# Second block of an attention and expert kernel: the six weight steps of a visit, each one step later

## The chip, the cores and the metric

The kernel runs on one core of a Trainium2 chip. The metric is the device time of one execution in microseconds (us). Before the change the median of three runs is 888.69 us (887.83 to 889.95).

## What is computed

A linear attention with random features is followed by a mixture of four experts. Batch 4, 8 heads, 576 positions, head size 64, 128 features. For queries and keys, `phi(x) = exp(h - max h)` with `h = x omega^T - |x|^2/2`; then `kv = phi(k)^T v`, `z = sum phi(k)`, and the attention output is `phi(q) kv / (phi(q) z + 1e-6)`. The 2304 rows of 512 columns that result are the input `x` of the experts: with `p` the normalised `domain_probs`,

```
out = sum over e of p[:, e] * (max(x @ w1[e], 0) @ w2[e])      w1: 4 x 512 x 1024, w2: 4 x 1024 x 512, fp32
```

## The kernel before

Every operand of a large product is split into a high and a low part (`hi` a rounded copy made by ScalarE, `lo` the rest, made by GpSimd or VectorE), and a product is three matmuls: high by high, high by low, low by high.

The experts' work is cut into visits: a block of rows times one half of one expert's hidden columns (8 halves). The first block of rows is done plainly (visits 0 to 10). The second block has 768 rows and the third 1024; both use a scheme of seven products in place of eight on 2 by 2 blocks, in `fast(v)`. Visits 11 to 18 are those of the second block, 19 to 26 ("deep") those of the third.

One visit of the second block runs in this order on TensorE (lines 1095 to 1170): products `p1(0) p2(0) p5(0) p6(0) p1(1) p2(1) p7(0) p5(1) p3(0) p4(0) p6(1)`, then `begun(0)`, `p7(1)`, `begun(1)`, `p3(1)`, `p4(1)`, `begun(2)`, and then six output tiles. A product is six matmuls of 384 columns (line 934), for chunk 0 or 1 of the hidden columns. An output tile is twelve matmuls of 512 columns (lines 753 to 755); `begun(t)` does the first six of tiles 0 to 2 early. Each product lands in a PSUM bank (eight banks, one pool for everything). `keep` (L940, ScalarE) copies `p1` out of a bank before `p6` is accumulated into that same bank; `both` (L946 on VectorE adds, L955 on ScalarE takes the positive part, L959 on VectorE the low part) makes the hidden operands. `gather` (L782, VectorE; L780, ScalarE, the first time) adds a finished tile to the output rows.

Beside this, three things are threaded in by hand; every engine works strictly in the order in which the code emits:

- `sides(v + 1)`, a generator with six steps (`ready`), which makes the next visit's operands of `w1` out of the two raw tiles `w1r`. `direct(0)` and `direct(1)` split three blocks of a raw tile as they are (`w1ah` by ScalarE L564, `w1al` by GpSimd L567); `add(0)`, `add(1)` make four combinations in place (four VectorE additions, L684 to L687); `summed(0)`, `summed(1)` split those (`w1sh` by ScalarE, `w1sl` by GpSimd) and then issue, on the queue of SP, one load of a raw `w1` tile for the visit after (L549). They run in the order `direct(0) direct(1) add(0) summed(0) add(1) summed(1)`. Each of the four operand tags has two buffers, one for each raw tile: `direct(0)` of the next visit writes where the operands of this visit lie.
- `keep_sides(v)` (L670), emitted after `p3(0)`: eight transfers that write this visit's operands from those same buffers to DRAM (`kept`), where the third block fetches them.
- `next(ticks)`: pieces of the attention of the last batch, some 1.2 a step, emitted at each `yield 1`, that is after `begun(2)` and after each output tile: projections, maxima (L282, L287), biases (L292, L293), exponentials (L299, L306), GpSimd squares (L251), reciprocals, loads.

Before the change the first step of `ready` runs between `p6(1)` and `begun(0)`, and the other five after output tiles 0 to 4; the call after tile 5 finds nothing left. In visit 18 (the last before the third block) the call ahead of `begun(0)` is not made.

Of the kernel before, what the change touches and what calls it, by code (L numbers as in the profile page):

```python
# [14 lines left out]
def attention_moe(ctx, tc, kT, qT, kd, qd, kn, qn, vn, omT, probs, w1, w2, out):  # L15
# [514 lines left out]
    DEEP = range(N0 + NV, len(visits))  # L530
# [361 lines left out]
    def fast(v):  # L892
# [6 lines left out]
        ready = sides(v + 1) if v + 1 < len(visits) else iter(())  # L899
# [78 lines left out]
        def p6(g):  # L978
            product(g, 6, "u", start=False)
            keep(g, "u", "u2")  # L980
# [19 lines left out]
        def begun(t):  # L1000
            g2[t] = bank("g2")
            outputs(v, hs, g2[t], t, range(2))
# [142 lines left out]
        if v + 1 == DEEP[0]:  # L1145
            start_sides2(v + 1)
        p6(1)
        if v + 1 != DEEP[0]:
            next(ready, None)
        begun(0)  # L1150
        p7(1)
        begun(1)
# [226 lines left out]
    def emit():  # L1379
        pairs, g1 = begin()  # L1380
        later = [Halves(b, hp) for b in range(1, B) for hp in range(NP)]
        windows = {
            0: (first_rest(pairs, opening(later[0], both=True)), 15 / 11),
            3: (joint_ticks(later[:-NP]), 76 / 45.4),
            N0: (chain(opening(later[-NP]), later_ticks(later[-NP:])), 54 / (NV * (BIG[1][1] // P + 1) * 0.8)),
        }
        ticks, n, done, per = iter(()), 0, 0.0, 0
        for v in range(len(visits)):
            if v in windows:
                for _ in ticks:  # L1390
                    pass
                ticks, per = windows[v]
                n, done = 0, 0.0
            for share in first_visit(g1) if v == 0 else fast(v) if v >= N0 else plain(v):
                done += share
                while n < done * per:
                    next(ticks, None)
                    n += 1
        store(0)
# [61 lines left out]
```

## Time and profile before

| | us |
|---|---|
| median of three runs | 888.69 |
| lowest, highest | 887.83, 889.95 |
| the profiled execution | 889.82 |
| its span, first to last instruction | 888.0 |
| granted TensorE clock | 1.000 |

The profile is of one execution. PE is TensorE's matmuls, DVE VectorE, ACT ScalarE, POOL GpSimd, SP the queue that issues most transfers (its instructions have names such as SPq). Times in the rows are from the start of the span; "L940" is a line of the kernel. A bracket at the end of a timeline row gives the idle time of the engine ahead of the row and what ended it.

### The profile page before, as it was taken

The numbers are of one execution on the slowest core, as the hardware profiler recorded it, in microseconds if no ns is written. First come the engines' busy times: TensorE is split into PE (matmuls) and PEld (weight loads), VectorE is DVE, ScalarE is ACT, GpSimd is POOL, SyncE is SP. The second block draws the span as 40 slices with busy tenths as digits, with TensorE's granted clock in tenths as the row PEclk, the third lists the DMA queues.
The fourth block names the chain that finished last, engine by engine and source line by source line (L and its number), as shares of the span: only waits on it lengthen the run. The fifth ranks groups of instructions, "written<-read, shape, count | busy, mean of one in ns | idle before, by whom it ended". The sixth has DMA issues, their size and how long they took to land.

```text
span 888.0 us, 14766 instructions
## 1 busy us (share of the span) xinstructions
PE 878.8 (99%) x5484; PEld 789.4 (89%) x5484; DVE 590.9 (67%) x1025; ACT 470.2 (53%) x1039; POOL 563.7 (63%) x494
## 2 busy tenths in 40 slices
PE   9999999999999989999999999999999999999998
PEld 9988888989888888989888899899989898998988
DVE  5765566666677556576766756975858476675847
ACT  6554677776774555555554554544443434444442
POOL 6656465555644454443545346779898887979874
PEclk9999999999999999999999999999999999999999
DMA  7675345444521847536375354644152442415132
GB/s 183 164 223 158 110 161 176 128 137 139 183 72 48 297 123 262 198 131 236 88 262 169 116 213 160 235 152 154 60 178 75 149 155 86 155 60 179 46 121 95
DMA packets 64296, 134.01 MB, mean 151 GB/s; under 512 B 10368, under 2 KB 20800, under 8 KB 64224
## 3 DMA queue, kind: packets, MB, share of 16 engines
q1 hardware_dynamic: 54256, 102.95, 35.3%
q0 software_dynamic: 9360, 29.82, 10.4%
q8 instruction: 43, 0.70, 0.3%
q10 hardware_dynamic: 608, 0.30, 0.1%
q14 instruction: 29, 0.24, 0.1%
HBM read 98.96 MB, written 34.08 MB: 150 GB/s over the span
## 4 chain that ended last, share of the span: by engine, by line
PE 92%; DVE 3%; DMA 2%; issue 1%; POOL 1%; ACT 1%; SPq 0%; POOLq 0%; ACTq 0%
PE g L934 28%; PE g L1009 18%; PE g L753 8%; PE g L755 7%; PE g L754 7%; PE g L738 3%; PE g L739 3%; PE g L740 3%; PE kv L317 2%; PE q_ps L266 1%; PE k_ps L266 1%; PE qt_ps L328 1%; PE k_ps L147 1%; DMA kept<-w1ah 1%; PE q_ps L147 1%
## 5 line engine op out<-in xcount | busy, mean ns | idle before, releaser
L782 DVE SCALAR_TENSOR_TENSOR acc<-g,pr,acc 128x256 f32<-128x256 f32 (+1 forms) x278 | 139.2, 540 | 37.0 <-PE g L755 27.5
L567 POOL TENSOR_TENSOR w2l<-w2r,w2h 128x512 fp32r<-128x512 f32 x61 | 79.3, 1305 | 80.4 <-ACT w2h L564 68.2
L567 POOL TENSOR_TENSOR w1sl<-w1r,w1sh 128x512 fp32r<-128x512 f32 (+1 forms) x43 | 75.1, 1747 | 64.3 <-ACT w1sh L564 53.4
L753 PE MATMUL g<-w2h,hh 128*128 128x512 f32 x280 | 112.0, 400 | 1.8 <-DVE sum L946 1.6
L755 PE MATMUL g<-w2h,hl 128*128 128x512 f32 x280 | 109.7, 392 | 0.0
L754 PE MATMUL g<-w2l,hh 128*128 128x512 f32 x280 | 109.5, 391 | 0.0
L959 DVE SCALAR_TENSOR_TENSOR hl<-sum,hh 128x384 fp32r<-128x384 f32 (+1 forms) x64 | 48.3, 757 | 81.5 <-ACT hh L955 71.7
L946 DVE TENSOR_TENSOR sum<-g,sum 128x384 f32<-128x384 f32 (+1 forms) x96 | 59.3, 619 | 61.2 <-PE g L934 52.8
L934 PE MATMUL g<-xbh,w1sh 128*128 128x384 f32 (+1 forms) x256 | 93.1, 364 | 2.4 <-ACT sum L940 2.4
L934 PE MATMUL g<-xbl,w1sh 128*128 128x384 f32 (+1 forms) x256 | 92.9, 363 | 0.0
L934 PE MATMUL g<-xbh,w1sl 128*128 128x384 f32 (+1 forms) x256 | 92.6, 362 | 0.0
L940 ACT ACTIVATE sum<-g 128x384 f32<-128x384 f32 (+1 forms) x96 | 52.1, 543 | 69.2 <-PE g L934 68.3
L567 POOL TENSOR_TENSOR w1al<-w1r,w1ah 128x512 fp32r<-128x512 f32 (+1 forms) x45 | 51.4, 1157 | 52.2 <-ACT w1ah L564 35.4
L934 PE MATMUL g<-xbh,w1ah 128*128 128x384 f32 (+1 forms) x192 | 70.0, 365 | 0.0
L934 PE MATMUL g<-xbl,w1ah 128*128 128x384 f32 (+1 forms) x192 | 69.6, 362 | 0.0
L934 PE MATMUL g<-xbh,w1al 128*128 128x384 f32 (+1 forms) x192 | 69.5, 362 | 0.0
L753 PEld LDWEIGHTS g<-w2h,hh 128*128 128x128 f32 x280 | 52.6, 188 | 12.7 <-DVE sum L946 2.2
L755 PEld LDWEIGHTS g<-w2h,hl 128*128 128x128 f32 x280 | 52.5, 188 | 11.8 <-DVE hl L992 0.4
L754 PEld LDWEIGHTS g<-w2l,hh 128*128 128x128 f32 x280 | 52.6, 188 | 9.0
L955 ACT ACTIVATE hh<-sum 128x384 fp32r<-128x384 f32 (+1 forms) x64 | 35.0, 548 | 43.9 <-DVE sum L946 43.5
L934 PEld LDWEIGHTS g<-xbh,w1sh 128*128 128x128 f32 x256 | 48.1, 188 | 8.4 <-ACT sum L940 2.7
L934 PEld LDWEIGHTS g<-xbl,w1sh 128*128 128x128 f32 x256 | 48.1, 188 | 5.1
(214 smaller groups left out, 2475.3 us busy)
## 6 DMA issues: line engine op xcount, KB each, us to landing
w1r<-in_w SPq DMA_DIRECT2D x54, 512.0 KB, 3.6
w2r<-in_w SPq DMA_DIRECT2D x76, 256.0 KB, 2.9
kept<-w1sh SPq DMA_DIRECT2D x16, 512.0 KB, 5.0
kept<-w1sl SPq DMA_DIRECT2D x16, 512.0 KB, 5.5
w1sh<-kept POOLq DMA_DIRECT2D x16, 512.0 KB, 4.7
w1sl<-kept POOLq DMA_DIRECT2D x16, 512.0 KB, 5.6
kept<-w1ah SPq DMA_DIRECT2D x16, 384.0 KB, 5.1
kept<-w1al SPq DMA_DIRECT2D x16, 384.0 KB, 5.0
```

Source lines behind the costliest of these rows:

```text
L567: lo.tensor_tensor(c, t, f32(a), ALU.subtract)
L738: nc.tensor.matmul(ps[:, :n], a[:, w], hi, start=(hp == 0), stop=False)
L753: nc.tensor.matmul(ps, ha[:, ts_], wa, start=(c == 0), stop=False)
L754: nc.tensor.matmul(ps, ha[:, ts_], wc, start=False, stop=False)
L755: nc.tensor.matmul(ps, hc[:, ts_], wa, start=False, stop=(c == FH - 1))
L782: nc.vector.scalar_tensor_tensor(to, ps, sc, to, ALU.mult, ALU.add)
L934: nc.tensor.matmul(ps, a[:, w], x[:, k], start=(start and k + at == 0), stop=(k == 1 and at == 2), skip_group_check=not start)
L940: nc.scalar.activation(t, P_[g][where], AF.Copy)
L946: nc.vector.tensor_tensor(t, P_[g][where], t, ALU.add)
L955: nc.scalar.activation(ha, t, AF.Relu)
L959: nc.vector.scalar_tensor_tensor(x, y, 0.0, f32(z), ALU.max, ALU.subtract)
L1009: nc.tensor.matmul(to, x, w, start=(start and f + k == 0), stop=(f + k == 3), skip_group_check=not start)
```

## The change

In visits 11 to 17 the call between `p6(1)` and `begun(0)` is taken out. As a step is still taken after every output tile, the same six steps now run after tiles 0 to 5: each comes one place later, with all that it issues (two ScalarE copies and two GpSimd subtractions for each `direct`, four VectorE additions for each `add`, one ScalarE copy, one GpSimd subtraction and one SP load for each `summed`). Visit 18 is as it was. TensorE's own order doesn't change.

```
         p6(1)
-        if v + 1 != DEEP[0]:
-            next(ready, None)
         begun(0)
         p7(1)
         begun(1)
```

## Rows read from the trace of the kernel before

**Rows 1.** Windows, three lines: visit 12, visit 16, the sum over visits 11 to 18
```profile
317.20:357.32 40.12, 37.75 (x217) 33.85 (x215) 22.99 (x42) 22.25 (x54) 18.15 (x13) 1.00 0.56 191
...
468.80:506.85 38.05, 36.45 (x205) 32.23 (x204) 24.82 (x44) 19.03 (x46) 15.47 (x12) 1.00 0.45 152
...
sum 286.35, PE 282.19 PEld 252.47 DVE 188.28 ACT 153.18 POOL 138.18; mean PE 35.27 PEld 31.56 DVE 23.53 ACT 19.15 POOL 17.27
```

**Rows 2.** Timeline of TensorE, visit 16 (start us, duration us, engine, line)
```profile
486.38 0.34 PE L934 MATMUL g<-xbh,w1al 128*128 128x384 f32 x1
488.32 0.50 PE L753 MATMUL g<-w2h,hh 128*128 128x512 f32 x1 [1.60 <-DVE sum L946]
488.66 0.40 PE L754 MATMUL g<-w2l,hh 128*128 128x512 f32 x1
```

**Rows 3.** Chain of work ahead of that matmul (start us, us, what)
```profile
479.82 5.14 DMA kept<-w1ah
...
486.45 1.34 DVE hl L959
487.79 0.48 DVE sum L946
```

**Rows 4.** Timeline of ScalarE, visit 16
```profile
485.07 0.94 ACT L564 ACTIVATE w1ah<-w1r 128x512 fp32r<-128x512 f32 x2 [3.68 <-DMA kept<-w1ah]
```

**Rows 5.** Timeline of VectorE, visit 16
```profile
483.27 0.56 DVE L946 TENSOR_TENSOR sum<-g,sum 128x384 f32<-128x384 f32 x1 [2.34 <-PE g L934]
```

**Rows 6.** Groups by form, visits 11 to 17 (xcount | busy us, mean ns | idle, releasers)
```profile
L564 ACT ACTIVATE w1ah<-w1r 128x512 fp32r<-128x512 f32 x14 | 8.9, 634 | 18.4 <-DMA kept<-w1ah 18.4
...
L564 ACT ACTIVATE w1sh<-w1r 128x1024 fp32r<-128x1024 f32 x14 | 14.8, 1060 | 19.4 <-issue 13.0 <-DVE w1r L687 6.4
...
L567 POOL TENSOR_TENSOR w1sl<-w1r,w1sh 128x1024 fp32r<-128x1024 f32 x14 | 34.2, 2442 | 37.5 <-ACT w1sh L564 27.6 <-issue 5.3 <-PE qt_ps L328 4.6
...
L687 DVE TENSOR_TENSOR w1r<-w1r 128x256 f32<-128x256 f32 x14 | 6.0, 425 | 0.5
...
L782 DVE SCALAR_TENSOR_TENSOR acc<-g,pr,acc 128x512 f32<-128x512 f32 x36 | 26.4, 739 | 12.1 <-PE g L755 11.9
...
L940 ACT ACTIVATE sum<-g 128x384 f32<-128x384 f32 x42 | 20.6, 491 | 14.3 <-PE g L934 13.6
```

**Rows 7.** Timeline of TensorE, visit 15
```profile
448.42 0.34 PE L934 MATMUL g<-xbh,w1al 128*128 128x384 f32 x1
448.75 0.50 PE L753 MATMUL g<-w2h,hh 128*128 128x512 f32 x1
```

**Rows 8.** Timeline of TensorE, visit 11
```profile
304.03 0.39 PE L754 MATMUL g<-w2l,hh 128*128 128x512 f32 x1
304.42 0.50 PE L755 MATMUL g<-w2h,hl 128*128 128x512 f32 x1
```

**Rows 9.** Timeline of TensorE, start of visit 12
```profile
322.89 0.45 PE L934 MATMUL g<-xbh,w1sh 128*128 128x384 f32 x1 [2.37 <-ACT sum L940]
```

**Rows 10.** Timeline of VectorE ahead of it, visit 11
```profile
316.59 2.32 DVE L293 SCALAR_TENSOR_TENSOR nbk<-sqk,mxk 128x9 f32<-128x9 f32 x1
```

**Rows 11.** Timelines, end of visit 17 and start of visit 18: POOL, DVE, PE
```profile
536.42 2.68 POOL L567 TENSOR_TENSOR w1sl<-w1r,w1sh 128x1024 fp32r<-128x1024 f32 x1 [2.88 <-ACT w1sh L564]
...
536.88 2.50 DVE L685 TENSOR_TENSOR w1r<-w1r 128x256 f32<-128x256 f32 x1
...
536.82 0.39 PE L753 MATMUL g<-w2h,hh 128*128 128x512 f32 x1
...
539.54 0.33 PE L934 MATMUL g<-xbh,w1ah 128*128 128x384 f32 x1
...
542.69 0.33 PE L934 MATMUL g<-xbh,w1sh 128*128 128x384 f32 x1
...
546.85 0.33 PE L934 MATMUL g<-xbh,w1sh 128*128 128x384 f32 x1
```

**Rows 12.** Chain of work over the whole span, the same transfer in visit 13
```profile
368.22 3.51 DMA kept<-w1ah
```

More of the change, by code (lines that the diff above doesn't have):

```diff
@@ L1147, in fast @@
         p6(1)
-        if v + 1 != DEEP[0]:
-            next(ready, None)
         begun(0)
```

## The prediction

> **What bounds the kernel now.** TensorE does. I read the windows by visit first: over visits 11 to 18 TensorE is busy 282.19 of 286.35 us, so 4.16 us of idle time is all that anything in these visits can win, and it lies in few places: visit 12 has 2.37 us of it and visit 16 has 1.60 [rows 1]. The rest is smaller than the profile counts as idle and must be read from starts: an unhindered product matmul follows the last after 0.175 us (18 of them between the start of visit 18 and its `p6(0)`, 542.69 - 539.54 [rows 11]), a tile matmul after 0.227 us (twelve between 536.82 and 539.54 [rows 11]).
>
> Then the stall of visit 16. The first matmul of `begun(2)` comes at 488.32, 1.94 us after the one ahead of it, released by VectorE's L946 [rows 2]. The chain behind it runs back over L959 to a transfer, `kept<-w1ah`, which is this visit's operand on its way to DRAM and took 5.14 us [rows 3]. Between the two is ScalarE: it stood 3.68 us with the two copies of `direct(0)` at its head, because they overwrite the buffer that this transfer reads [rows 4]. All ScalarE work behind them had to wait, first the positive part of `p7(1)`, whose sum VectorE had finished at 483.83 [rows 5]. VectorE, also in order, then did `p7(1)`'s low part (L959, 1.34 us from 486.45) ahead of `p3(1)`'s sum, and that sum frees the bank that `begun(2)` wants [rows 3]. In all ScalarE lost 18.4 us in nine such waits [rows 6]; most cost TensorE nothing, but visit 15 shows a start 0.33 us after the last and visit 11 one of 0.39 at the matmul that needs the last low part [rows 7, 8].
>
> The other stall, 2.37 us at `p6(0)` of visit 12, is of another kind: `keep` (L940) is late on ScalarE [rows 9], because the attention's exponentials stand ahead of it, which waited for a bias (L293) that took 2.32 us [rows 10].
>
> **The change, part by part.** It removes no instruction; six steps in each of visits 11 to 17 come one place later.
>
> *`direct(0)`, from before `begun(0)` to after tile 0.* The two copies leave the head of ScalarE at the critical place. By then `begun(0)` to `begun(2)`, three products and half a tile have passed: 18 product matmuls (3.15 us) and 24 tile matmuls (5.4 us), 8.6 us, more than the 5.14 us of the slowest transfer shown. So the wait is gone, not moved. In visit 16 `p7(1)`'s positive part could start at 483.83 instead of about 486.0 (485.07 + 0.94 [rows 4]), `p3(1)`'s sum follows its product, and `begun(2)` follows after 0.175. Gain: 488.32 - 486.38 - 0.175 = 1.77 us, and the slow first matmul behind the stall (488.66 - 488.32 = 0.34 against 0.227), 0.11 us [rows 2]. Visit 15: 0.33 - 0.175 = 0.16 us [rows 7]. Visit 11: 0.39 - 0.227 = 0.16 us [rows 8]. Together 2.20 us. On GpSimd the two `w1al` subtractions go along; they no longer run beside L959.
>
> *`direct(1)`, after tile 1, and `add(0)`, `summed(0)` after tiles 2 and 3.* I cost these at nothing. Cover: the next visit needs `w1ah` of chunk 1 only at `p1(1)`, more than four tiles of 2.72 us later. `summed(0)` (1.06 on ScalarE, then 2.44 on GpSimd [rows 6]) starts two tiles before the visit ends and is wanted at `p5(0)`, 12 matmuls into the next one: 5.4 + 2.1 = 7.5 us for 3.5 us of work. Without that cover each microsecond late would be one of TensorE's.
>
> *`add(1)` after tile 4, `summed(1)` after tile 5.* This is the tight one, and what is late next. `add(1)` follows tile 4's gather on VectorE: tile 4 ends 2.72 us before the visit does, the gather takes 0.74, the four additions 4 x 0.46 = 1.84 (0.425 and a gap of 0.5 / 14) [rows 6], so they end 0.1 us before the next visit starts. `summed(1)`'s copy (1.06) now stands on ScalarE straight ahead of the next visit's `keep` (0.49), which `p6(0)` needs 3.15 us into the visit: 1.55 after -0.1 is 1.45, a margin of 1.7 us. Its low part (2.44) ends at about 3.4 us, against `p5(1)` at 546.85 - 539.54 = 7.3 us [rows 11]: margin 3.9 us. It also pushes the first `w2l` of the next visit back on GpSimd; those are first read by `begun(0)`, eleven products (11.5 us) in.
>
> At the end of visit 17 the margin fails narrowly. VectorE's second addition took 2.50 us there and not 0.425, for as long as GpSimd's `w1sl` of the other chunk (2.68 us from 536.42) ran [rows 11]. Shifted, that subtraction starts some 0.4 us later (behind one gather more, 0.74, less what was idle) and ends at about 539.5; all four additions then wait for it: 539.5 + 1.84 + 1.06 + 0.49 = 542.9 against `p6(0)` at 542.69. Cost 0.2 us. The Trainium skill, "SBUF — State Buffer", section "SBUF: two separate sides", states this as a rule: VectorE with two SBUF inputs and GpSimd share an exclusive lock, and the loser is blocked for the whole instruction. The trace agrees, with that 2.50 beside 2.68; by the rule alone every `add(1)` that meets a `w1sl` would lose up to 2.44 us, which is the second rival below.
>
> *Queues.* SP's raw-tile load goes along with each `summed` (twelve, from visits 11 to 16); it waits there for `w1sl`, and `w2r` loads and some of the attention's loads stand behind it. The `w2r` loads wait for GpSimd work that is behind `w1sl` anyway, and a raw tile is not read for a whole visit (35.8 us on average [rows 1]). Cost nothing. `kept` transfers keep their place. On GpSimd the attention's squares now go ahead of the `w1sl` that they followed.
>
> *Visit 12's stall: unknown, bounded from both sides.* It can vanish: the bias is late by 2.32 us beside `w1sl` of chunk 1, which leaves that place; then -2.37 us. It can grow by `summed(1)`'s copy, 1.06 us, which now stands between the exponentials and `keep` [rows 6, 9, 10]. I take 0: some of the 2.32 us is given back (chunk 0's `w1sl` moves in), and about as much as the copy costs.
>
> **Sum.** -2.20 + 0.20 + 0 = -2.0 us, so 887.8 for the profiled execution (889.82: the span of 888.0 and 1.82 around it). That execution lies 1.13 us above the median; against the median, 888.69 - 2.0 = **886.7 us**.
>
> **Rivals.** *1, the stall is this execution's own.* `kept<-w1ah` took 5.14 us in visit 16 but 3.51 in visit 13 [rows 3, 12]. With 3.51 ScalarE would have started 1.63 us sooner and the stall been 0.14, as in visit 15. The gain is then 0.14 + 0.16 + 0.16 - 0.2, about 0.3 us: 888.4, no change. For it: the median lies 1.13 us lower. Against it: nothing between the visits' programs differs but what is fixed by the order, so the same meeting of transfers should come again. Chance 0.21.
>
> *2, slower: `add(1)` held by GpSimd at every visit's end, so that `keep` is late and `p6(0)` stalls.* Place: the first 3.15 us of visits 12 to 18. Held the whole 2.44 us, the additions end 2.3 us into the visit, the copy and `keep` at 3.9, so `p6(0)` loses 0.7 us. Seven times that is 4.9 us, less 2.2: 891.4. It decides from the fourth visit on (2.2 / 0.7) and shows as slower from the sixth. For it: visit 17. Against it: in an unhindered visit `add(0)`, the copy and `w1sl` of chunk 0 take 1.84 + 1.06 + 2.44 = 5.34 us, and between the gathers of tiles 2 and 4 lie two tiles, 5.44; it just fits, and visits with attention matmuls between the tiles have more room. Chance 0.12.
>
> *3, more: visit 12's stall goes too.* 2.0 + 2.37: 884.3. For it: the long bias is gone if GpSimd is idle when it runs. Against it: the copy is in the way. Chance 0.15.
>
> **The numbers.** The forecast has 0.52, and by its own rows 885.6 to 887.8 (visit 12 by about 1 us either way). A measurement of this kernel can tell about 0.2%, 1.78 us, from no change, so the forecast of -2.0 lies just beyond: 0.34 of it as faster, 0.18 as same. Rival 3 adds 0.14 to faster and 0.01 to same, rival 1 0.21 to same, rival 2 0.10 to slower and 0.02 to same. Faster 0.48, same 0.42, slower 0.10. The range 885.0 to 889.0 holds the forecast, rival 1 and the smaller half of rival 3, and leaves out some 0.18.
>
> **What would show it.** Right: no wait of ScalarE's `w1ah` copies for `kept<-w1ah`; in visit 16 `begun(2)` within 0.2 us of `p4(1)`; L959 of `p7(1)` well below its 1.34 us. `keep` (L940) of each visit straight after `w1sh`, ending before 3.15 us; a new idle time at `p6(0)` that names ScalarE's L940 would show rival 2, its absence in visit 12 rival 3. The prediction is wrong if visit 16's stall stays, or if the idle time of TensorE over these visits isn't about 4.2 - 1.6 us, some 2.6.

## The result, and the profile after

The changed kernel takes 892.59 us (median of six runs, 889.98 to 893.43), the kernel before 887.47 in the same comparison: a ratio of 1.0051 (95% interval 1.0032 to 1.0070). The change makes it slower by half a per cent; the prediction said 886.7 and is wrong. The profiled execution took 893.14 us, its span is 891.4.

Visits 11 to 18 are where the time went: they take 288.88 us, 286.21 in the profile of before, and the part behind them 317.92 against 317.49. Windows of the changed kernel, from each visit's first product to the next one's (us from:to, length, busy time of PE, PEld, DVE, ACT, POOL, granted clock, DMA share, GB/s); the lines are visits 12, 15, 16, 18 and the sum, and answer to [rows 1]:

```profile
317.66:356.20 38.54, 37.75 (x217) 33.84 (x216) 21.78 (x43) 22.20 (x53) 16.26 (x13) 1.00 0.58 202
...
429.11:468.28 39.17, 37.73 (x217) 33.85 (x216) 27.25 (x44) 21.80 (x50) 16.58 (x12) 1.00 0.52 184
468.28:508.62 40.34, 37.72 (x205) 33.82 (x204) 25.86 (x46) 19.35 (x47) 15.43 (x13) 0.96 0.42 147
...
541.31:573.45 32.14, 31.32 (x158) 28.08 (x156) 23.44 (x30) 18.80 (x30) 21.77 (x21) 1.00 0.70 251
sum 288.88, PE 282.78 PEld 253.73 DVE 192.73 ACT 152.97 POOL 135.96; mean PE 35.35 PEld 31.72 DVE 24.09 ACT 19.12 POOL 17.00
```

Visit 12 is 1.6 us shorter than in the profile of before (a second profile of that kernel, `g4` below, says otherwise), visits 15 and 16 are 1.2 and 2.3 longer, and only in visit 16 is the granted clock below 1. TensorE is idle for 6.10 us (288.88 - 282.78), where the prediction said some 2.6. Its waits in the changed kernel (line waited for: us in all, times, longest):

```profile
PE g L934 <- DVE sum L946: 4.1, 2, 2.6
PE g L934 <- ACT sum L940: 1.6, 2, 0.8
```

The wait of `begun(2)` (L753) in [rows 2] is gone, and so is ScalarE's for `kept`: among its groups by form in visits 11 to 18 the `w1ah` copies now have next to no idle time ahead of them, against 18.4 us in [rows 6]:

```profile
L564 ACT ACTIVATE w1ah<-w1r 128x512 fp32r<-128x512 f32 x14 | 8.9, 636 | 0.1
```

In their place stand waits of the products themselves. The largest is at `p2(1)` of visit 16 (timeline of TensorE):

```profile
473.44 0.34 PE L934 MATMUL g<-xbh,w1al 128*128 128x384 f32 x1
476.40 0.44 PE L934 MATMUL g<-xbh,w1ah 128*128 128x384 f32 x1 [2.62 <-DVE sum L946]
...
477.23 0.52 PE L934 MATMUL g<-xbh,w1ah 128*128 128x384 f32 x1
477.55 0.52 PE L934 MATMUL g<-xbl,w1ah 128*128 128x384 f32 x1
...
480.11 0.37 PE L934 MATMUL g<-xbh,w1sh 128*128 128x384 f32 x1
```

The wait costs 476.40 - 473.44 - 0.175 = 2.79 us. Behind it the matmuls start 0.32 us apart and not 0.175, until 480.11: twelve of them take 3.71 us in place of 2.10, another 1.61. The windows show why (columns as above; the clock is the number after the five engines):

```profile
476.40:478.40 2.00, 2.00 (x7) 2.00 (x8) 0.56 (x1) 0.50 (x1) 0.00 (x0) 0.59 0.60 198
478.40:480.40 2.00, 2.00 (x8) 2.00 (x8) 0.61 (x2) 0.52 (x1) 0.00 (x0) 0.56 0.00 0
480.40:482.40 2.00, 2.00 (x13) 2.00 (x12) 1.53 (x3) 1.42 (x3) 0.34 (x1) 1.00 0.00 0
```

TensorE had stood for 2.62 us, and for the next 4 us it ran mostly at the lower of its two levels (1.2 GHz; 0.5 would be all of it), then at 2.4 GHz again. With the like wait at `p2(1)` of visit 15 (436.05 after 434.27: 1.61 us), `p6(0)` of visit 12 (321.76 after 320.63: 0.96) and of visit 18 (545.45 after 544.29: 0.99), that makes 1.61 + 2.79 + 1.61 + 0.96 + 0.99 = 7.96 us. The best kernel below, whose profile has no such wait, takes 280.80 us for these visits; 288.88 - 280.80 = 8.08, so the list holds nearly all of it (a wait of 0.42 us for a load, ahead of a projection at 310.75 in visit 11, is not in it).

**Where `p2(1)` of visit 16 waits.** It wants a bank, and the one that it gets is freed by VectorE's L946, the sum of `p2(0)`. VectorE of the changed kernel, end of visit 15 and start of visit 16 (which begins at 468.28):

```profile
464.80 1.22 DVE L684 TENSOR_TENSOR w1r<-w1r 128x256 f32<-128x256 f32 x1
466.06 0.42 DVE L685 TENSOR_TENSOR w1r<-w1r 128x256 f32<-128x256 f32 x1
...
466.97 0.42 DVE L687 TENSOR_TENSOR w1r<-w1r 128x256 f32<-128x256 f32 x1
467.32 1.74 DVE L368 RECIPROCAL dn<-dn 128x256 f32<-128x256 f32 x1
...
469.55 2.14 DVE L368 RECIPROCAL dn<-dn 128x320 f32<-128x320 f32 x1
...
473.38 1.16 DVE L292 SCALAR_TENSOR_TENSOR mxk<-sqk,mxk 128x9 f32<-128x9 f32 x1
474.57 1.18 DVE L293 SCALAR_TENSOR_TENSOR nbk<-sqk,mxk 128x9 f32<-128x9 f32 x1
475.79 0.56 DVE L946 TENSOR_TENSOR sum<-g,sum 128x384 f32<-128x384 f32 x1
```

The same place in the kernel before (visit 16 begins at 468.80; `add(1)` had ended at 464.8):

```profile
468.28 2.14 DVE L368 RECIPROCAL dn<-dn 128x320 f32<-128x320 f32 x1
...
472.11 0.60 DVE L292 SCALAR_TENSOR_TENSOR mxk<-sqk,mxk 128x9 f32<-128x9 f32 x1
472.75 0.17 DVE L293 SCALAR_TENSOR_TENSOR nbk<-sqk,mxk 128x9 f32<-128x9 f32 x1
472.95 0.56 DVE L946 TENSOR_TENSOR sum<-g,sum 128x384 f32<-128x384 f32 x1
```

Counted from the visit's start, L946 began at 4.15 us in the kernel before and begins at 7.51 us now, 3.36 later. That splits exactly: the second reciprocal starts 1.27 us into the visit and not 0.52 ahead of it (1.79, as `add(1)` now stands straight ahead of the reciprocals), L292 takes 1.16 and not 0.60 (0.56), L293 1.18 and not 0.17 (1.01). `p2(1)` is due 5.33 us in, so VectorE had 0.6 us to spare before (4.15 + 0.56 = 4.71). The last two parts are GpSimd's, and 0.8 us of the first (L684 took 1.22 and not 0.42), in the changed kernel:

```profile
463.33 2.41 POOL L567 TENSOR_TENSOR w1sl<-w1r,w1sh 128x1024 fp32r<-128x1024 f32 x1 [1.50 <-ACT w1sh L564]
...
473.24 2.49 POOL L567 TENSOR_TENSOR w2l<-w2r,w2h 128x512 fp32r<-128x512 f32 x2
```

L684, three times as long as the additions behind it, ends 0.28 us after `w1sl` (466.02, 465.74); L292 and L293, of nine columns, each end with one of the two `w2l` (474.5 and 475.7), which come so late because `w1sl` of chunk 1 ran ahead of them (470.04 to 472.44). The Trainium skill, "SBUF — State Buffer", section "SBUF: two separate sides", has VectorE with two SBUF inputs and GpSimd shut each other out for a whole instruction; these rows agree.

**`p6(0)` of visit 18**, in the changed kernel (GpSimd, VectorE, ScalarE, TensorE), answers to [rows 11]:

```profile
539.85 2.69 POOL L567 TENSOR_TENSOR w1sl<-w1r,w1sh 128x1024 fp32r<-128x1024 f32 x1 [2.42 <-ACT w1sh L564]
...
540.32 2.50 DVE L685 TENSOR_TENSOR w1r<-w1r 128x256 f32<-128x256 f32 x1
...
543.82 1.06 ACT L564 ACTIVATE w1sh<-w1r 128x1024 fp32r<-128x1024 f32 x1 [4.04 <-DVE w1r L687]
544.90 0.49 ACT L940 ACTIVATE sum<-g 128x384 f32<-128x384 f32 x1
...
545.45 0.44 PE L934 MATMUL g<-xbh,w1sh 128*128 128x384 f32 x1 [0.82 <-ACT sum L940]
```

This is the chain of the prediction, addition held, copy, `keep`, `p6(0)`.

### The profile page after: what moved, and what is told of

Its sections match the earlier page's. It is cut to its first block, busy times and chain, and to the rows that moved or that the text cites. A ratio compares the mean times of both kernels' runs of the same rounds, so it can differ in the third digit from the quotient of the medians.

```text
span 891.4 us, 14767 instructions
## 1 busy us (share of the span) xinstructions
PE 879.3 (99%) x5484; PEld 790.1 (89%) x5484; DVE 594.9 (67%) x1025; ACT 469.7 (53%) x1039; POOL 562.6 (63%) x494
## 4 chain that ended last, share of the span: by engine, by line
PE 90%; DVE 6%; ACT 1%; DMA 1%; issue 1%; POOL 1%; SPq 0%; POOLq 0%; ACTq 0%; DVEq 0%
PE g L934 29%; PE g L1009 18%; PE g L753 7%; PE g L754 7%; PE g L755 7%; PE g L738 3%; PE g L739 3%; PE g L740 3%; PE kv L317 2%; PE q_ps L266 1%; PE qt_ps L328 1%; PE k_ps L266 1%; DVE dn L368 1%; DVE acc L782 1%; PE kv L177 1%
## 5 line engine op out<-in xcount | busy, mean ns | idle before, releaser
L753 PE MATMUL g<-w2h,hh 128*128 128x512 f32 x280 | 111.7, 399 | 0.0
L946 DVE TENSOR_TENSOR sum<-g,sum 128x384 f32<-128x384 f32 (+1 forms) x96 | 59.4, 621 | 65.6 <-PE g L934 62.1
L959 DVE SCALAR_TENSOR_TENSOR hl<-sum,hh 128x384 fp32r<-128x384 f32 (+1 forms) x64 | 43.0, 675 | 71.1 <-ACT hh L955 47.7
L940 ACT ACTIVATE sum<-g 128x384 f32<-128x384 f32 (+1 forms) x96 | 52.1, 543 | 64.4 <-PE g L934 63.5
L753 PEld LDWEIGHTS g<-w2h,hh 128*128 128x128 f32 x280 | 52.7, 188 | 10.1
```

The costliest lines, as they stand in the source:

```text
L753: nc.tensor.matmul(ps, ha[:, ts_], wa, start=(c == 0), stop=False)
L940: nc.scalar.activation(t, P_[g][where], AF.Copy)
L946: nc.vector.tensor_tensor(t, P_[g][where], t, ALU.add)
L959: nc.vector.scalar_tensor_tensor(x, y, 0.0, f32(z), ALU.max, ALU.subtract)
```

## The experiments

Each edit is shown against the changed kernel. The tuple gives how many steps of `ready` run after output tiles 0 to 5; behind the first of these hunks only the line with the tuple is shown. The expectations name theories of the loss: "lock", "queue" and "copy" are spelt out in that of `e3`, "meeting" (lock and queue together) in that of `f1`. The kernels ran in several comparisons, each beside the kernel before, so ratios are compared ahead of times. "The extra call" is this hunk, one step straight behind `begun(2)`:

```
         begun(2)
+        if v + 1 != DEEP[0]:
+            next(ready, None)
         yield 1
```

**Undoing most of it.** `e4`: the extra call, and

```
-            next(ready, None)
+            for _ in range((1, 1, 1, 1, 1, 0)[t] if v + 1 != DEEP[0] else 1):
+                next(ready, None)
```

so only `direct(0)` has moved, and only as far as `begun(2)`.

> Only direct(0) moves (behind begun(2)); the other five steps stay where the kernel before has them. All theories of the loss (lock, queue, copy) say that it comes from the steps behind direct(0): they expect the stall of 1.6 us in visit 16 gone, no stall of the kernel after (visits 15, 16, 18) and a time 1.8 to 2.4 us below the kernel before. Rival: any shift of the visits makes such stalls; then one of over 1 us shows at p2(1) or p6(0) of some visit, and the time is that of the kernel before or more.

884.56 us, ratio 0.9983 (0.9971 to 0.9996). The gain that the prediction counted is there, and the time is what the theories expected (2.25 us less by the medians). Its profile has one long wait left, 2.5 us at `p6(0)` of visit 12, of the kind that the rival named; but the profiled execution took 886.91 us, and ten of the twelve took 883.76 to 884.91, so that wait is not the rule.

`e3`: the call between `p6(1)` and `begun(0)` put back, and only `summed(1)` late:

```
+            for _ in range((1, 1, 1, 1, 0, 1)[t] if v + 1 != DEEP[0] else 1):
```

> Only summed(1) moves, from tile 4 to tile 5; direct(0) to add(1) as in the kernel before. Theory lock (GpSimd's w1sl of chunk 1 runs at the start of the next visit and holds VectorE's bias steps, which stand ahead of the sum that frees p2(1)'s bank): stalls at p2(1) of visits 15 and 16 of 0.5 us or more, time 1 to 4 us above the kernel before (the stall of visit 16 behind direct(0) stays). Theory queue (VectorE's additions stand behind one more gather, GpSimd is incidental): additions are where they were, so no stall at p2(1), time within 0.5 us of the kernel before. Theory copy (w1sh ahead of keep on ScalarE): a stall at p6(0) of up to 1 us in some visits, none at p2(1).

886.89 us, ratio 1.0005 (0.9990 to 1.0021): `summed(1)` alone costs nothing that can be told, as "queue" expected and "lock" did not. `begun(2)` of visit 16 waits 0.9 us again.

`e2`: the change, with `summed(1)` behind tile 4, right after `add(1)`:

```
+            for _ in range((1, 1, 1, 1, 2, 0)[t] if v + 1 != DEEP[0] else 1):
```

> The kernel after with summed(1) back behind tile 4, right behind add(1). Theory lock: the copy waits for add(1) anyway, so w1sl of chunk 1 starts within 0.3 us of the kernel after; stalls of visits 15 and 16 within 0.5 us of the kernel after, time 3 to 5 us above the kernel before. Theory copy: the copy leaves the place ahead of keep, so the time falls to the kernel before less about 2 us. Theory queue: as the kernel after.

896.30 us, ratio 1.0108 (1.0093 to 1.0122): worse, and by more than any of the theories expected. `w1sh` of chunk 1 then stands on ScalarE ahead of the attention's exponentials and waits there for the late additions (ahead of visit 12 they stand behind a bias, L292, held for 2.19 us); `p6(0)` waits up to 3.4 us for L940. So to take the copy from its place ahead of `keep` wins nothing; earlier is worse as long as its additions are late.

**Parts of it, with `direct(0)` behind `begun(2)`.** `f1`: the extra call, `add(1)` and `summed(1)` late:

```
+            for _ in range((1, 1, 1, 0, 1, 1)[t] if v + 1 != DEEP[0] else 1):
```

> direct(0) behind begun(2); direct(1), add(0), summed(0) where the kernel before has them; only add(1) and summed(1) a tile later (tiles 4 and 5), as in the kernel after. Theory meeting (VectorE's additions of chunk 1 behind one more gather push its queue into the next visit, where GpSimd's w1sl and w2l of chunk 1 then hold the bias steps; the sum behind them frees p2(1)'s bank): stalls at p2(1) of visits 15 and 16, 1 us or more each, time 889 to 893, near the kernel after. Rival early (the move of add(0) and summed(0) is what fills VectorE's and GpSimd's queues): no such stall, time 884 to 886.

886.89 us, ratio 0.9996 (0.9987 to 1.0005). Against `e4` the pair gives, by the medians, nearly the whole gain back (the intervals overlap). "Meeting" expected two waits and 889 to 893 us, its rival none: one came. The profile shows `p2(1)` of visit 16 waiting for the same sum; L946 starts 6.02 us into the visit (471.17 - 465.15):

```profile
471.79 0.44 PE L934 MATMUL g<-xbh,w1ah 128*128 128x384 f32 x1 [1.14 <-DVE sum L946]
```

`f2`: the extra call, `add(0)` and `summed(0)` late, chunk 1 in place:

```
+            for _ in range((1, 0, 1, 2, 1, 0)[t] if v + 1 != DEEP[0] else 1):
```

> direct(0) behind begun(2); add(0) and summed(0) a tile later (tiles 2 and 3), add(1) and summed(1) where the kernel before has them (tiles 3 and 4). Theory meeting: no stall at p2(1), time 884 to 886, as with direct(0) alone. Rival early: stalls at p2(1) of visits 15 and 16 of 1 us or more, time 889 to 893.

887.07 us, ratio 1.0004 (0.9988 to 1.0020). The other pair does the same one visit sooner: `p2(1)` of visit 15 waits 1.0 us, where one expectation was no wait and the other was waits in two visits. These are the steps that the prediction costed at nothing.

`f6`: the extra call, only `summed(1)` late:

```
+            for _ in range((1, 1, 1, 1, 0, 1)[t] if v + 1 != DEEP[0] else 1):
```

> direct(0) behind begun(2) and summed(1) behind tile 5, add(1) and the rest as in the kernel before. The two runs that moved one of them alone had, the first, no stall in visit 16 but 2.5 us at p6(0) of visit 12, the second 0.2 us there but the stall of visit 16. If they add up: neither, time 882 to 884, below both kernels. Rival: summed(1)'s place makes a new stall at p2(1) of visits 15 or 16 once visit 16 no longer waits, time 885 or more.

885.91 us, ratio 0.9982 (0.9970 to 0.9993): as good as `e4` within the intervals, with about 1.0 us each at `p2(1)` of visit 16 and `p6(0)` of visit 12. The two moves don't add up; the rival came true.

`g1`: the extra call, all four additions and sums late, `direct(1)` in place:

```
+            for _ in range((1, 0, 1, 1, 1, 1)[t] if v + 1 != DEEP[0] else 1):
```

> direct(0) behind begun(2) and direct(1) behind tile 0, so both ahead of where the kernel after has them; add(0), summed(0), add(1), summed(1) behind tiles 2 to 5, as in the kernel after. Theory meeting: the two pairs moved alone cost one stall of about 1.1 us each (visit 15 or 16); together they use up VectorE's room at the end of both visits, so stalls at p2(1) of 15 and 16 and over 0.5 us at p6(0) of visit 18, time 889 to 893, near the kernel after. Rival directs (the two w1al subtractions, a tile later on GpSimd, push everything behind them): no more than one stall of 1.3 us, time 885 to 888.

889.03 us, ratio 1.0021 (1.0010 to 1.0032): both waits at `p2(1)` (1.4 and 1.2 us) and 1.0 at visit 12's `p6(0)`, but no low clock, and no wait in visit 18, where "meeting" expected one. Less than half of the change's loss.

`f5`: the change, with the attention's step behind tile 5 taken only after the next visit's `begun(2)`:

```
         begun(2)
-        yield 1
+        yield 1 if v == N0 else 2
...
-            yield 1
+            if t + 1 < tiles:
+                yield 1
         for _ in more:
```

> The kernel after, but the attention pieces that follow tile 5 are emitted behind begun(2) of the next visit, so that neither the bias steps nor the four banks of a projection stand at the start of visits 15 and 16. Theory meeting: the stalls at p2(1) of visits 15 and 16 and the low clock behind the second go; p6(0) of visit 18 keeps about 1 us (no attention there); time 4 to 7 us below the kernel after. Rival (the steps' own work, without the attention, fills the queues): stalls of over 1 us stay at p2(1) or p6(0) of visits 15 and 16, time within 2 us of the kernel after.

888.97 us, ratio 1.0020 (1.0007 to 1.0032), 2.8 us below the change by the ratios and 3.1 by the medians, each against the kernel before of its own comparison; 4 to 7 was expected. Both waits at `p2(1)` and the low clock are gone, as the attention no longer has a projection with its maxima and biases across the visit's start. Waits of `p6(0)` for L940 stay, up to 1.1 us, one of them new (visit 15). That `p2(1)` waits for this very sum because the projection holds four of the eight banks is read from the code; a kernel that frees a bank there was not tried.

**The direct steps.** `g2`: only they are late, as the change has them, with `add(0)` behind `direct(1)` and the rest in place:

```
+            for _ in range((1, 2, 1, 1, 1, 0)[t] if v + 1 != DEEP[0] else 1):
```

> direct(0) and direct(1) behind tiles 0 and 1, where the kernel after has them; add(0) right behind direct(1), summed(0), add(1), summed(1) behind tiles 2 to 4, as in the kernel before. Theory meeting: no stall at p2(1) and none in visit 16, time 884 to 886, as with direct(0) alone. Rival directs: stalls as in the kernel after in at least one visit, over 1.3 us, time 887 or more.

894.05 us, ratio 1.0079 (1.0065 to 1.0092): by the median worse than the whole change, though the intervals touch. The theory that only the additions and sums lose the time falls. `p2(1)` of visit 16 waits 1.38 us, with the additions in place. Visit 12's `p6(0)` waits 4.34 us, and the granted clock behind it is 0.50, 0.50 and 0.81 in three windows of 2 us:

```profile
324.52:326.50 1.98, 1.98 (x6) 1.98 (x7) 0.54 (x1) 1.36 (x3) 1.44 (x2) 0.50 0.04 8
326.50:328.50 2.00, 2.00 (x7) 2.00 (x7) 0.00 (x0) 0.49 (x1) 1.07 (x1) 0.50 0.48 130
328.50:330.50 2.00, 2.00 (x11) 2.00 (x11) 0.74 (x2) 0.91 (x2) 0.00 (x0) 0.81 0.51 132
```

Three more kernels ask which of the two it is. `e1`: `direct(0)` and `direct(1)` behind tile 0, the rest in place:

```
+            for _ in range((2, 1, 1, 1, 1, 0)[t] if v + 1 != DEEP[0] else 1):
```

> Edit: only direct(0) moved, behind tile 0 where the change puts it, with direct(1) right behind it; everything else as before the change. Theory 'direct(1)': direct(0)'s place behind tile 0 costs nothing and takes visit 16's wait away: 884 to 886 us (ratio 0.997 to 0.999). Rival 'direct(0)': 889 us or more (ratio over 1.0025).

890.78 us, ratio 1.0046 (1.0029 to 1.0063). The expectation of the theory "direct(1)" fails: with nothing but `direct(0)` moved from behind `begun(2)` (`e4`) to behind tile 0 (one step of the attention and half a tile later), the kernel goes from 0.17% faster to 0.46% slower. In the profile it all happens at visit 12's `p6(0)`. The timelines of `e1` (GpSimd, VectorE, ScalarE, TensorE, and the window behind the wait, with the clock third from its end):

```profile
312.84 2.58 POOL L567 TENSOR_TENSOR w1sl<-w1r,w1sh 128x1024 fp32r<-128x1024 f32 x1
...
316.92 2.40 POOL L567 TENSOR_TENSOR w1sl<-w1r,w1sh 128x1024 fp32r<-128x1024 f32 x1 [0.21 <-ACT w1sh L564]
...
313.19 2.51 DVE L687 TENSOR_TENSOR w1r<-w1r 128x256 f32<-128x256 f32 x1
...
318.11 1.23 DVE L292 SCALAR_TENSOR_TENSOR mxk<-sqk,mxk 128x9 f32<-128x9 f32 x1
...
319.58 0.74 ACT L306 ACTIVATE kp<-t_ps,nbk 64x128 f32<-64x128 f32 x2 [2.74 <-DVE nbk L293]
...
322.91 0.55 ACT L940 ACTIVATE sum<-g 128x384 f32<-128x384 f32 x1
...
323.51 0.59 PE L934 MATMUL g<-xbh,w1sh 128*128 128x384 f32 x1 [3.38 <-ACT sum L940]
...
323.51:325.50 1.99, 1.99 (x7) 1.99 (x8) 0.54 (x1) 1.37 (x3) 1.45 (x2) 0.53 0.04 8
```

An addition held for 2.51 us by one `w1sl`, a bias held for 1.23 by the other, exponentials that wait for the bias, `keep` behind them, and a clock of 0.53 behind the wait: the stall of [rows 9, 10] again, a microsecond longer, and this time with the clock.

`h1`: the extra call, only `direct(1)` late, with `add(0)` right behind it:

```
+            for _ in range((0, 2, 1, 1, 1, 0)[t] if v + 1 != DEEP[0] else 1):
```

> Edit: direct(0) behind begun(2), direct(1) behind tile 1 with add(0) right behind it, everything else as before the change. Theory 'direct(1)': VectorE's and GpSimd's queues have no room behind tile 1, because GpSimd's low part of chunk 1 then stands behind the attention's work and add(0), w1sl and w2l come after it, beside VectorE's bias steps; then this kernel loses what the two directs together lost: 892 to 894 us (ratio 1.005 to 1.008), with a stall over 2 us at p6(0) of visit 12 and one over 1 us at p2(1) of visit 16. Rival 'direct(0)': direct(1)'s place is free and it is direct(0) behind tile 0 that costs: then 884 to 886 us, as with direct(0) alone behind begun(2).

886.55 us, ratio 1.0001 (0.9987 to 1.0016); neither theory's number. By the medians it gives `e4`'s gain back and no more (the intervals overlap). Its profiled execution, at 891.66 us, is its slowest, and the only one of the twelve with a mean granted clock as low as 0.998: there `p6(0)` of visit 12 waited 2.43 us and the clock fell. The other wait that the theory "direct(1)" named is in it too, at `p2(1)` of visit 16 (which begins at 470.50), with `add(0)` to `summed(1)` in place:

```profile
477.31 0.44 PE L934 MATMUL g<-xbh,w1ah 128*128 128x384 f32 x1 [1.32 <-DVE sum L946]
```

In the other executions, about 5 us shorter, the mean clock was 0.999 or 1.000.

`h3`: the whole change, with `direct(1)` back behind tile 0:

```
+            for _ in range((2, 0, 1, 1, 1, 1)[t] if v + 1 != DEEP[0] else 1):
```

> Edit: the whole change, but direct(1) right behind direct(0) after tile 0, where it was before. Theory 'direct(1)': its place is what the whole change loses beyond its additions, so this kernel falls to that of the additions alone: 888 to 889.5 us (ratio 1.001 to 1.003), with no fall of the granted clock behind visit 16's p2(1). Rival 'direct(0)': nothing changes against the whole change, 891 to 893 us.

888.88 us, ratio 1.0030 (1.0018 to 1.0042), as the theory "direct(1)" expected, and with no fall of the clock. In visit 16 `add(1)` is not held (four additions of 0.42), the second reciprocal starts 0.24 us ahead of the visit (467.29, 467.53) where the change has it 1.27 into it, and L946 starts 6.01 us in and not 7.51. So in the whole change the place of `direct(1)` is worth 1.5 us at `p2(1)`, and the low clock behind it. The two direct steps lose time at different places, `direct(0)` in visit 12 (`e1`), `direct(1)` in visit 16, with the additions late (`h3` against the change) or in place (`h1`, `g2`). Neither is "the" cause.

**The hold by itself.** `e5`: the change, with each `w1sl` in four pieces:

```
-            split(tiles[i], sh, sl, nc.scalar, nc.gpsimd)
+            nc.scalar.activation(sh, tiles[i], AF.Copy)
+            for j in range(4):
+                cs = slice(j * H, (j + 1) * H)
+                nc.gpsimd.tensor_tensor(sl[:, cs], tiles[i][:, cs], f32(sh[:, cs]), ALU.subtract)
```

> The kernel after with each w1sl subtraction (128x1024) cut into four of 128x256; more GpSimd time (about 2.9 us for 2.4), same order. Theory lock: VectorE gets in between the pieces, a bias step is held at most about 0.7 us in place of 1.2, and the additions of visit 17 0.7 in place of 2.5; the stalls at p2(1) of visits 15 and 16 shrink by half or more, p6(0) of visit 18 by 1 us; time 2 to 4 us below the kernel after. Theory queue or copy: stalls as in the kernel after within 0.3 us.

887.54 us, ratio 1.0011 (1.0003 to 1.0020) where the change has 1.0051, with the same order of the steps: 3.6 us less by the ratios, 4.4 by the medians. "Lock" expected 2 to 4. It is still no faster than the kernel before. In visit 16 of `e5` VectorE shows (the visit begins at 466.91)

```profile
467.35 2.14 DVE L368 RECIPROCAL dn<-dn 128x320 f32<-128x320 f32 x1
...
471.18 0.36 DVE L292 SCALAR_TENSOR_TENSOR mxk<-sqk,mxk 128x9 f32<-128x9 f32 x1
471.57 1.21 DVE L293 SCALAR_TENSOR_TENSOR nbk<-sqk,mxk 128x9 f32<-128x9 f32 x1
472.81 0.56 DVE L949 TENSOR_TENSOR sum<-g,sum 128x384 f32<-128x384 f32 x1
```

The reciprocal starts 0.44 us into the visit and not 1.27, and the bias is 0.36 and not 1.16: the sum (L949 here) begins 5.90 us in and not 7.51. L293 is still held, by `w2l`, which was not cut. The waits of visits 15 (now at `p5(1)`) and 16 are about 1.0 us each, that of `p6(0)` in visit 18 is gone, and no clock falls.

`g3`: the hunks of `e4` and of `e5` together.

> direct(0) behind begun(2), all else as before, and each w1sl subtraction cut into four. If GpSimd's long subtraction is what holds the bias ahead of visit 12's p6(0), the stall there falls from 2.5 us to under 1 us, and no stall over 0.5 us is left: time 882 to 884, below both kernels and below direct(0) alone. Rival: the extra GpSimd time (0.5 us each, 14 times) or the late load of k sets that stall; time as with direct(0) alone, 884 to 885.

885.16 us, ratio 0.9971 (0.9959 to 0.9983): faster than both kernels, though not the 882 to 884 expected. Its waits of TensorE name no product any more:

```profile
PE warm L1191 <- DVE om_r L1182: 1.1, 1, 1.1
PE q_ps L266 <- DVE qtl L339: 0.7, 1, 0.7
```

`e4` and `g3` are not told apart by their intervals; what `g3` adds is that visit 12's wait is gone and that its eleven runs lie within 883.97 to 885.71, `e4`'s twelve within 883.76 to 889.56.

**The kernel before, once more** (`g4`, no edit):

> The kernel before, for a second profile of it. If the stall of visit 16 belongs to the program, begun(2) there stands still 1 us or more again; if it belonged to the one execution (the transfer of 5.14 us), the transfer takes 3.5 to 4 us and the stall is under 0.5 us. Time: no change.

887.01 us, ratio 0.9997 (0.9979 to 1.0015). Visit 16's wait comes again, shorter than the 1.60 of [rows 2]; visit 12's 2.37 of [rows 9] does not, and visits 11 to 18 take 283.01 us, not 286.21.

```profile
485.92 0.50 PE L753 MATMUL g<-w2h,hh 128*128 128x512 f32 x1 [1.26 <-DVE sum L946]
```

Against this second profile the change costs 5.87 us in these visits, 1.61 of it at the low clock: visits 12, 15, 16 and 18 are longer by 1.10, 1.33, 2.70 and 1.13, visit 13 is shorter by 0.62. Why visit 12 waited in one profile of the same program and not in the other can be read from GpSimd and VectorE (GpSimd of before; VectorE and GpSimd of `g4`):

```profile
316.49 2.40 POOL L567 TENSOR_TENSOR w1sl<-w1r,w1sh 128x1024 fp32r<-128x1024 f32 x1
...
316.35 0.17 DVE L293 SCALAR_TENSOR_TENSOR nbk<-sqk,mxk 128x9 f32<-128x9 f32 x1
...
317.15 2.40 POOL L567 TENSOR_TENSOR w1sl<-w1r,w1sh 128x1024 fp32r<-128x1024 f32 x1 [0.86 <-ACT w1sh L564]
```

In the first profile `w1sl` starts 0.10 us ahead of the bias (316.59 [rows 10]) and the bias takes 2.32 us; in `g4` the bias comes first and takes 0.17. Against the start of visit 12 (317.20 and 317.95) `w1sl` stands at the same place, within 0.1 us, and the bias a whole microsecond earlier in `g4`, as do the squares that it follows (L251), for which both profiles name the load of `q` as what they waited for. `e4` and `h1` have the unlucky order in their profiles (`w1sl` at 316.49 and 317.31, the bias at 316.60 and 317.41, 2.32 us each).

In the changed kernel the bias ahead of visit 12 (L293) takes 0.17 us as well, but the copy of `summed(1)` stands among the exponentials, ahead of `keep` (ScalarE; the visit begins at 317.66):

```profile
319.21 1.08 ACT L564 ACTIVATE w1sh<-w1r 128x1024 fp32r<-128x1024 f32 x1
```

**The clock over all runs.** The mean granted clock of the whole span sorts most of the runs. Of the change's six runs five had 0.997 or 0.998 and took 892.19 to 893.43 us; the sixth had 1.000 and took 889.98. `e1` had 0.996 to 0.998 in all nine runs, `g2` 0.996 or 0.998 in all four. `h3`, `g1` and `f5`, the change with one or two of its parts undone, had 0.999 or 1.000 in every run and took about 889 us. The kernel before has it too: in the comparisons of the experiments 16 of its 116 runs had 0.997 or 0.998 and took 889.01 to 892.15 us, the other 100 took 884.19 to 889.52. The clock is not everything: one run of `f2` took 890.24 us at 1.000. So the 5.1 us of the change are, by these runs, some 2.5 us of waits (889.98 - 887.47, one run; `h3`, `g1` and `f5` have 2.0 to 2.4 over theirs) and some 2.6 to 3.2 of what a longer wait and its low clock add.

## Why the prediction was wrong

- **What bounds the kernel; the gain.** Right. ScalarE's wait for `kept` is gone and with it the stalls of visits 16, 15 and 11. By the runs of `e4` the move of `direct(0)`, as far as `begun(2)`, is worth 0.17%, 1.5 us (2.25 by the medians), where the sum said 2.20; the profiled 1.60 of visit 16 was at the upper end of what comes again (1.26 and 0.9), and 0.6 us in visit 13 were not in the sum.
- **"`direct(1)`, and `add(0)`, `summed(0)` ... I cost these at nothing."** This step failed. The cover was computed from when TensorE reads the operands, and there it held: no product waited for one. It left out who stands behind the moved steps on VectorE and GpSimd. `f2` shows the one pair worth a wait of 1.0 us at `p2(1)` of visit 15, `h1` that `direct(1)` alone gives back `e4`'s gain by the medians and makes a wait of 1.32 us at `p2(1)` of visit 16, and `h3` that in the whole change its place is worth 1.5 us there. The place of `direct(0)`, too, was taken as free anywhere behind `begun(2)`; `e1` shows that behind tile 0 it is not.
- **"`add(1)` after tile 4, `summed(1)` after tile 5. This is the tight one."** The right steps, the wrong victim. The margin of 1.7 us was that of `keep` and `p6(0)`. Behind `add(1)` on VectorE stand the attention's reciprocals, maxima and biases and then the sum that frees `p2(1)`'s bank, with 0.6 us to spare; that chain was in the trace and the prediction followed it only as far as `keep`.
- **Visit 18.** The chain held, the size did not: 0.99 us and not 0.20. `w1sl` was to begin 0.4 us later and began 1.66 later by the visit's own time (539.85 - 541.31 against 536.42 - 539.54), because it hangs on `add(0)`. That starts 0.66 us later, about the gather that was counted, but its first two additions (L684, L685) then take 1.41 and 0.84 us and not 0.82 and 0.42, beside `w1al` of `direct(1)` (two from 535.27, 2.17 us), which the sum had at nothing.
- **Visit 12, taken as 0.** In the profile its wait fell from 2.37 to 0.79, and both bounds were at work: the bias took 0.17 us, and the copy of `summed(1)`, 1.08 us from 319.21, stood among the exponentials, ahead of `keep`. But 2.37 was that one execution's (`g4` has no such wait), so what looks like a gain of 1.6 us was luck of the first profile, and beside `g4` visit 12 loses 1.10. Rival 1, put on visit 16's stall, holds for this one. The place is the most easily upset of all: 0.3 in `f1`, 1.3 in `h3`, 2.5 in `e4`, 3.38 in `e1`, 4.34 in `g2`.
- **Rival 2** had part of the cause, VectorE and GpSimd shutting each other out, at a chance of 0.12, but mostly the wrong instruction and place: it looked for `add(1)` at `p6(0)` of seven visits. `add(1)` was held ahead of visit 16 (L684, 0.8 us) and of visit 18 (L685, 2.1 us), and only in visit 18 did that reach `p6(0)`. At `p2(1)` of visits 15 and 16 the biases were held (L292 and L293, 1.24 and 1.20 us in visit 15), behind additions that came a tile later.
- **The granted clock** stood at 1.00 in the profile of before and had no term. It took 1.61 us in the profile of after; with the longer wait ahead of it, it is what separates 889 from 893.
- **Open.** The effects don't add: the direct steps alone (`g2`) lose no less than with the rest late as well, and `e1`, which moves one step only, loses nearly as much. The traces show which instruction is held by which in the visits read here, but no run gives a rule by which the meetings of a new order could be foretold.

## What to carry to other kernels

When a step is moved later, follow each engine's own queue behind it, not only the operand that it makes: ask which instruction stands next on VectorE and GpSimd, and which bank it frees. Where the cover is spare time on an engine that shares with GpSimd, cut the long GpSimd instructions first, then move: with the order unchanged `e5` took back 0.40 of the change's 0.51%, though by itself it won nothing over the kernel before. Before a sum rests on a wait of one profile, take a second (`g4`). And judge a wait at TensorE by its length as well as by the sum: several of one microsecond cost what they show, one of two and a half or more sometimes cost half as much again.

## What was not expected of the hardware

A nine-column instruction of VectorE, 0.17 us by itself, took 1.18 us in the changed kernel, until one GpSimd instruction of 1.25 (2.49 / 2) had ended, and 2.32 in [rows 10], beside a `w1sl` of 2.40: the length was set by GpSimd's instruction, not by VectorE's own work, and whether it is paid hung on which of the two started first, by 0.10 us in [rows 10]. And the clock fell after one wait of 2.62 us (0.59 and 0.56 in the next two windows), 2.43 (`h1`), 3.38 (0.53), 3.41 (`e2`: 0.87, 0.50, 0.78) or 4.34 (0.50, 0.50, 0.81), but not after the 2.51 in `e4` (1.00 in the three windows of 2 us behind it), nor after any shorter one read here.
